# Bias and residual of a GFNet block: an fp32 home for every tile, filled by ScalarE and one accumulating DMA, and more idle matmuls before the first dense one

## The chip, the cores and the metric

The kernel runs on one core of a Trainium2 chip. A core has five engines with a queue each: TensorE (PE, with its weight loads as PEld), VectorE (DVE), ScalarE (ACT), GpSimd (POOL) and SyncE (SP), besides 16 DMA engines. Each engine works through its own queue in order and waits there on semaphores. The metric is the device time of one execution in microseconds, measured by timing whole executions. The profile comes from one further execution, which the hardware profiler recorded.

## The reference

With `x` of shape 1 x 2048 x 640 in bf16, the block is

```python
xn  = _layernorm(x)                                   # over the 640 columns
X   = rfft2(xn) * (w_r + 1j * w_i)                    # 2048 x 321 filter
y   = irfft2(X, s=(2048, 640)).astype(bfloat16)
h   = gelu(xn @ w1 + b1)                              # 640 -> 1536, tanh form
out = x + y + (h @ w2 + b2)                           # 1536 -> 640
```

## The kernel before

The 2048 rows are cut into 16 tiles of 128 rows (tile c holds the rows 16p + c, one on each partition p). The kernel has five stages, and they overlap.

1. **Norm.** DVE takes the statistics of a tile (L559, L561), POOL forms the reciprocal root (`rstd`, L564), DVE forms `nmr` (L566) and the normalised tile (`T<-X,rstd,nmr`, L587). TensorE transposes it (L599, `ps<-ident,T`), and ACT or DVE copies the result into `xnT`.
2. **First dense layer.** `ps<-xnT,W` multiplies `xnT` by `w1`; ACT applies the gelu with its bias (L645) and writes `gT`. The first two tiles go alone (128 columns), then pairs (256 columns), then two groups of four tiles (512 columns).
3. **Spectrum.** The discrete transform is written as matmuls: along the rows inside a tile (`ps<-gtab,T`, into `XV`), along the columns (`ps<-etab,XV`, into `Xb`), the remaining radix (`ps<-Xb,mtab`, into `Y`), the filter on DVE (L704, L708), and back (`ps<-Z,ntab`, into `gtab` and `T`, then a transposing DMA of SP into `XV`, L732). The stage `ps<-etab,XV` needs all 16 tiles.
4. **Back along the columns.** `ps<-getab,XV`, ACT and DVE into `Wf`, then sums and differences on DVE (L754, L759).
5. **Final sums.** For each tile the second dense layer (`ps<-W,gT`, 24 matmuls) and the last part of the inverse transform (`ps<-Wf,htab`, 2 matmuls) add up in two banks of PSUM. DVE (L819) adds an fp32 tile that holds bias plus residual, b2 + x, writes bf16 into a staging tile in `W`, and SP sends it out (L822).

Four tiles (`KEEP`) have their second dense layer done early, in the gaps of the spectrum stage. DVE then adds the bias and parks the sum in fp32 in the storage of `xnT` (L808), and an accumulating DMA on POOL adds x there (L810). For the twelve others two DMAs on POOL build b2 + x: the first writes the bias, read 128 times from HBM, into one of **three** fp32 slots in the storage of `w1` (L784), the second accumulates x on top (L785, which waits for the first to land). A slot is free for the next tile only after the DVE addition (L819) that reads it. Both DMAs wait for the end of the first dense layer, because the slots lie where `w1` was.

The order on each engine is not written by hand. A planner simulates the whole program with rough durations, picks the next operation of each engine by start time and priority, and writes the resulting order into the queues. Its priorities, `AHEAD` and `LAG` set how far the stages run ahead of one another. The order is thus fixed at build time; on the chip an engine never takes a later operation first.

At the beginning 30 matmuls on a zeroed tile (`ps<-warm`) run before any input has landed. All loads are issued by SP one after another from 0.74 us on; the bias row `b2bc` (b2, broadcast to 128 partitions) is the last of them.

Of the kernel before, what the change touches and what calls it, by code (L numbers as in the profile page):

```python
# [8 lines left out]
F32 = dt.float32  # L9
ACT = mybir.ActivationFunctionType  # L10
ALU = mybir.AluOpType

S = 2048
D = 640
# [76 lines left out]
def mm_us(n):  # L91
    return max(n / 2400.0 + 0.0027, 0.0265)
# [6 lines left out]
def act_us(n, ptr=0):  # L99
    return 0.055 + n / 1200.0 + 0.09 * ptr  # L100
# [57 lines left out]
class Sched:  # L158
# [36 lines left out]
    def schedule(self):  # L195
        free = {e: 0.75 for e in self.engines}
        dma_free = 0.0
# [22 lines left out]
        while left:  # L220
            best = None
            for e in self.engines:
                cands = []
                for o in pend[e]:
# [17 lines left out]
                    t = max(r, free[e])  # L242
# [7 lines left out]
                if e == "sp":  # L250
                    t, o = min(cands, key=lambda c: c[1].seq)
                    if o is not min((p for p in pend[e] if not p.done), key=lambda p: p.seq):
                        continue
                else:
# [4 lines left out]
                    t, o = min(near, key=lambda c: (-c[1].prio, c[1].seq))  # L259
# [4 lines left out]
            t, e, o = best  # L264
# [8 lines left out]
            if o.nbytes:  # L273
                s = max(t + 0.9, dma_free)
                dma_free = s + o.nbytes / o.rate
                o.end = dma_free + 0.9
            else:
                o.end = t + dur + LAT[e]
# [104 lines left out]
LAG = 2  # L383
KEEP = (0, 1, 4, 6)


def bass_parallel_sum__spectral_gfnet__dense_activation_gelu__prompt_kernel(
# [13 lines left out]
    xv = A_x[0].rearrange("(p c) d -> p c d", c=16)  # L401
# [4 lines left out]
    b2v = B_b2.rearrange("(o e) -> o e", o=1)  # L406

    K = Sched(nc, ["sp", "pe", "act", "dve", "pool"])
    with ExitStack() as es:
# [51 lines left out]
        p_yo, p_y2, p_yf, p_xo, p_os = Pool(2), Pool(1), Pool(2), Pool(3), Pool(4)  # L461

# [109 lines left out]
        for pair in range(8):  # L572
# [10 lines left out]
            for n in range(2):  # L583
# [13 lines left out]
                def xt(e, _, n=n, xnv=xnv, tps=tps):  # L597
                    for j in range(5):
                        ins = e.transpose(psb(tps.slot, [[1, 512]]).bitcast(BF)[:, 128 * j:128 * j + 128], xnv(n, 128 * j, [[1, 128]]), ident[:])  # L599
                    return ins  # L600
                K.op([("pe", 5 * mm_us(128))], pr, xt, reads=[B_xn, xn, B_id], writes=[tps], alts=[[("128", 5 * mm_us(128))]])
                K.op([("dve", 0.41), ("act", act_us(640))], pr,
# [139 lines left out]
        for gi, (c0, n) in enumerate(GROUPS):  # L742
# [20 lines left out]
            for i in range(n):  # L763
                c = c0 + i
                kept = c in KEEP
                xo, os_ = Buf(f"xo{c}", None if kept else p_xo), Buf(f"os{c}", p_os)
# [12 lines left out]
                def shaped(ap, kept=kept):  # L779
                    return ap.rearrange("p (j t) -> p j t", j=5) if kept else ap  # L780
                b2d = bass.AP(tensor=b2v.tensor, offset=b2v.offset, ap=[[0, 128], [1, D]])
                if not kept:
                    xb2 = Buf(f"xz{c}")
                    K.op([("pool", 1.0)], 50, lambda e, _, xov=xov: e.dma_start(xov(0, D), b2d), writes=[xo, xb2], after=free, nbytes=327680, rate=330e3)  # L784
                    K.op([("pool", 1.0)], 51, lambda e, _, c=c, xov=xov: e.dma_start(xov(0, D), xv[:, c, :], accum_op=ALU.add),  # L785
                         reads=[xb2], writes=[xo], nbytes=327680, rate=250e3)

# [16 lines left out]
                if kept:  # L804
                    kps = Buf(f"kps{c}", psum, 2, ZONE["fps"])
                    second(c, kps, 0, D, pr, [kept_ops[-2]] if len(kept_ops) > 1 else [pb_ops[-2]])
                    kx = Buf(f"kx{c}")
                    kept_ops.append(K.op([("dve", dve_us(D))], 30, lambda e, _, kps=kps, xov=xov, shaped=shaped: e.tensor_tensor(  # L808
                        out=xov(0, D), in0=shaped(psb(kps.slot, [[1, D]])), in1=shaped(b2bc[:]), op=ALU.add), reads=[kps, B_b2b], writes=[kx], after=free))
                    K.op([("pool", 1.0)], 51, lambda e, _, c=c, xov=xov, shaped=shaped: e.dma_start(xov(0, D), shaped(xv[:, c, :]), accum_op=ALU.add),  # L810
                         reads=[kx], writes=[xo], nbytes=327680, rate=250e3)
                for o0, w in [(0, D)] if c < 15 else [(0, H2), (H2, Q4), (H2 + Q4, Q4)]:
# [43 lines left out]
```

## Time and profile before

| | us |
|---|---|
| median of 3 runs | 167.04 |
| lowest and highest run | 166.98 and 167.77 |
| the profiled execution, timed | 167.08 |
| its span, first to last instruction | 165.3 |
| the time around the span | 1.8 |
| mean granted TensorE clock | 0.994 |

| engine | busy us | share of the span |
|---|---|---|
| TensorE matmul | 151.5 | 92% |
| VectorE | 112.3 | 68% |
| ScalarE | 79.9 | 48% |
| GpSimd | 30.2 | 18% |

In the timelines a row gives the start, the time to the end of the last instruction, the engine, the line, the operation with its tiles and how many were merged; the bracket is the idle time before it and what ended it. Since matmuls are pipelined, the time from one group's start to the next group's start tells their pace better than the busy time does.

### The profile page before, as it was taken

How to read it: one execution, taken by the hardware profiler on the slowest of the kernel's cores; microseconds unless marked ns; L12 is line 12 of the kernel's file. 1: busy time of each engine (PE TensorE's matmuls, PEld its weight loads, DVE VectorE, ACT ScalarE, POOL GpSimd, SP SyncE). 2: the span in 40 equal slices, each digit the busy share in tenths (PEclk: the TensorE clock that was granted, in tenths of full speed). 3: DMA queues.
4: the chain of work that ended last, by engine and by line, in shares of the span. 5: the costliest groups of instructions: out<-in, count | busy, mean ns of one | idle time of the engine just before them, and what ended most of it. 6: DMA issues, size and time to landing. Idle time of an engine off the chain costs nothing.

```text
span 165.3 us, 3751 instructions
## 1 busy us (share of the span) xinstructions
PE 151.5 (92%) x1552; PEld 100.0 (60%) x1552; DVE 112.3 (68%) x254; ACT 79.9 (48%) x146; POOL 30.2 (18%) x45
## 2 busy tenths in 40 slices
PE   7399999999999999999999999999999999998422
PEld 7199999999764545455455454756655565444312
DVE  1694999999997499898899941799964151510302
ACT  3279999899877776966483514445030010000000
POOL 1202101110020000000040333433222405125020
PEclk9999999999999999999999999999999999999997
DMA  5999999999400001822837589679897485685941
GB/s 147 356 384 396 202 160 164 159 204 367 161 0 0 0 4 40 75 48 53 111 56 107 90 154 163 124 200 269 228 204 193 102 247 127 181 207 146 236 122 40
DMA packets 29816, 25.73 MB, mean 156 GB/s; under 512 B 12520, under 2 KB 25576, under 8 KB 29800
## 3 DMA queue, kind: packets, MB, share of 16 engines
q1 hardware_dynamic: 23064, 15.66, 41.5%
q0 software_dynamic: 6080, 9.18, 25.6%
q10 hardware_dynamic: 656, 0.66, 1.1%
q8 instruction: 12, 0.20, 0.6%
q14 instruction: 4, 0.03, 0.1%
HBM read 15.66 MB, written 2.62 MB: 111 GB/s over the span
## 4 chain that ended last, share of the span: by engine, by line
PE 60%; DMA 21%; issue 6%; DVE 6%; POOL 3%; ACT 2%; SPq 1%; DVEq 0%; POOLq 0%
PE ps L469 57%; DMA W<-in_B_b_dram 16%; PE ps L599 3%; POOL W L785 3%; DMA b1t<-in_B_b_dram 3%; DMA W<-in_A_x_dram 2%; DVE W L819 2%; DVE Wf L754 1%; DVE Wf L481 1%; ACT Wf L480 1%; SPq L464 1%; DVE T L481 1%; DVE Wf L759 0%; ACT xnT L480 0%; POOL W L784 0%
## 5 line engine op out<-in xcount | busy, mean ns | idle before, releaser
L469 PE MATMUL ps<-W,gT 128*128 128x512 bf16 (+3 forms) x396 | 56.5, 295 | 7.5 <-DVE W L819 7.5
L469 PE MATMUL ps<-xnT,W 128*128 128x256 bf16 (+2 forms) x420 | 58.8, 298 | 0.8 <-ACT xnT L480 0.8
L469 PEld LDWEIGHTS ps<-W,gT 128*128 128x128 bf16 x396 | 30.1, 98 | 31.0 <-DVE W L819 9.0
L469 PEld LDWEIGHTS ps<-xnT,W 128*128 128x128 bf16 x420 | 36.9, 103 | 16.0 <-issue 1.8
L645 ACT ACTIVATE gT<-ps,b1col 128x256 bf16<-128x256 f32 (+2 forms) x84 | 39.9, 506 | 8.6 <-PE ps L469 6.4
L819 DVE TENSOR_TENSOR W<-ps,W 128x640 bf16<-128x640 f32 (+2 forms) x14 | 10.1, 728 | 28.7 <-DMA W<-in_A_x_dram 19.0
L480 ACT ACTIVATE Wf<-ps 128x960 bf16<-128x960 f32 (+1 forms) x9 | 7.9, 910 | 22.4 <-PE ps L469 22.4
L559 DVE BATCH_NORM_STATS2 stats<-X 128x6 f32<-128x320 bf16 x32 | 14.5, 476 | 3.0 <-DMA X<-in_A_x_dram 3.0
L785 POOL DMA_DIRECT2D W<-in_A_x_dram x12 | 10.4, 871 | 31.4 <-DMA W<-in_B_b_dram 31.3
L810 POOL DMA_DIRECT2D xnT<-in_A_x_dram x4 | 6.2, 1544 | 48.7 <-DVE xnT L808 48.7
L564 POOL TENSOR_TENSOR rstd<-ve,mhalf 128x2 f32<-128x2 f32 (+1 forms) x9 | 6.4, 708 | 39.9 <-DVE ve L563 39.9
L704 DVE TENSOR_TENSOR T<-Y,Wf 128x1288 bf16<-128x1288 bf16 x16 | 12.7, 825 | 0.5 <-ACT Y L480 0.2
L480 ACT ACTIVATE Xb<-ps 128x960 bf16<-128x960 f32 (+1 forms) x6 | 6.8, 1138 | 6.5 <-PE ps L469 6.5
L784 POOL DMA_DIRECT2D W<-in_B_b_dram x12 | 8.3, 751 | 7.4 <-DVE W L819 4.5
L612 DVE TENSOR_TENSOR T<-T 128x512 bf16<-128x512 bf16 (+1 forms) x32 | 8.6, 320 | 0.0
L480 ACT ACTIVATE Y<-ps 128x644 bf16<-128x644 f32 x11 | 7.4, 715 | 1.9 <-PE ps L469 1.9
L480 ACT ACTIVATE xnT<-ps 128x640 bf16<-128x640 bf16 x8 | 5.4, 704 | 5.3 <-PE ps L599 5.3
L754 DVE TENSOR_TENSOR Wf<-Wf 128x960 bf16<-128x960 bf16 (+1 forms) x12 | 6.8, 599 | 1.6 <-ACT Wf L480 1.3
L469 PE MATMUL ps<-getab,XV 32*128 32x160 bf16 (+1 forms) x128 | 7.5, 241 | 0.0
L481 DVE CAST Xb<-ps 128x960 bf16<-128x960 f32 (+1 forms) x6 | 6.7, 1123 | 1.1 <-PE ps L469 1.1
L608 DVE TENSOR_TENSOR T<-T 128x640 bf16<-128x640 bf16 x16 | 7.3, 463 | 0.0
L469 PEld LDWEIGHTS ps<-getab,XV 32*128 32x128 bf16 (+1 forms) x128 | 6.5, 146 | 1.3
(45 smaller groups left out, 144.4 us busy)
## 6 DMA issues: line engine op xcount, KB each, us to landing
W<-in_B_b_dram POOLq DMA_DIRECT2D x12, 320.0 KB, 5.4
W<-in_A_x_dram POOLq DMA_DIRECT2D x12, 320.0 KB, 4.4
out_dram<-W SPq DMA_DIRECT2D x15, 160.0 KB, 2.8
X<-in_A_x_dram SPq DMA_DIRECT2D x7, 320.0 KB, 9.5
W<-in_B_w_dram SPq DMA_DIRECT2D x1, 1920.0 KB, 15.4
W<-in_B_w_dram SPq DMA_DIRECT2D x2, 640.0 KB, 7.1
xnT<-in_A_x_dram POOLq DMA_DIRECT2D x4, 320.0 KB, 5.0
Wf<-in_A_w_r_dram SPq DMA_DIRECT2D x7, 160.5 KB, 10.9
```

Source lines behind the costliest of these rows:

```text
L469: ins = e.matmul(o_, lhsT=lw, rhs=rh, start=st, stop=sp_, skip_group_check=True)
L480: return e.activation(dst(), src(), ACT.Copy, scale=scale)
L481: return e.tensor_copy(dst(), src())
L559: K.op([("dve", 0.393)], pr, lambda e, _, c=c, h=h: e.bn_stats(stats[:, c, 6 * h:6 * h + 6], view(X, c * D + H2 * h, [[1, H2]])), reads=[B ...
L608: K.op([("dve", dve_us(640, 2))], pr, lambda e, _, k=k, op=op, xnv=xnv, x1v=x1v: e.tensor_tensor(out=x1v(H2 * k, [[D, 2], [1, H2]]), in0=x ...
L612: ring_ops.append(K.op([("dve", dve_us(4 * w, 2))], pr, lambda e, _, op=op, x1v=x1v, xfv=xfv, o_=o_, o0=o0, o1=o1, w=w: e.tensor_tensor(ou ...
L645: K.op([("act", act_us(128 * nt, 1))], pr + PRIO["gelu"], lambda e, _, c0=c0, nt=nt, fc=fc, hps=hps: e.activation(gT[:, fc, 128 * c0:128 * ...
L704: filt_ops.append(K.op([("dve", dve_us(4 * KP, 2))], pr, lambda e, _, k=k, Y=Y, TB=TB, pair=pair: e.tensor_tensor(out=view(TT, TB.slot * 8 ...
L754: K.op([("dve", dve_us(320 * n, 2))], pr + 2, lambda e, _, k=k, op=op, yo=yo, y2=y2, n=n: e.tensor_tensor(out=view(Wf, Y2 + y2.slot * 3 * ...
L784: K.op([("pool", 1.0)], 50, lambda e, _, xov=xov: e.dma_start(xov(0, D), b2d), writes=[xo, xb2], after=free, nbytes=327680, rate=330e3)
L785: K.op([("pool", 1.0)], 51, lambda e, _, c=c, xov=xov: e.dma_start(xov(0, D), xv[:, c, :], accum_op=ALU.add), reads=[xb2], writes=[xo], nb ...
L819: K.op([("dve", dve_us(w))], 95, lambda e, _, os_=os_, fps=fps, o0=o0, w=w, xov=xov, shaped=shaped, base=base: e.tensor_tensor(out=shaped( ...
```

## The change

Four things are changed together.

- The fp32 slots in the storage of `w1` are gone. Each of the 16 tiles has an fp32 home of its own, eight in the storage of `xnT` (`HOME`) and eight in that of `X`, whose bf16 input is no longer needed once both tiles there are normalised. The output staging moves to the start of `w1`'s storage.
- The bias of a tile that isn't kept is written by an ACT copy from `b2bc` (priority 5, the lowest), no longer by a DMA. One accumulating DMA on POOL then adds x. The DMA needs only the home to be free, so the planner puts most of them far ahead of the finals.
- The kept tiles are 1, 3, 5 and 7 instead of 0, 1, 4 and 6, and the planner's model of a DMA on POOL is 5 us from its issue, apart from the other queue.
- The idle matmuls at the beginning are 55 instead of 30, and 12 more stand between the first tile's transposes and the first dense matmul (`WARM`).

```diff
-KEEP = (0, 1, 4, 6)
+KEEP = (1, 3, 5, 7)
+HOME = KEEP + tuple(range(15 - (8 - len(KEEP)), 15))
+WARM = (55, 12)
...
-        xot = W1[:].bitcast(F32)
-        OST = 3 * 2 * D
+        OST = 0
...
-        B_wps = Buf("warmps", psum)
-        pe([("128", 30 * 0.108)], 300, lambda: [(psb(B_wps.slot, [[1, 128]]), warm[:], warm[:], True, True) for _ in range(30)],
-           reads=[B_warm], writes=[B_wps])
+        def idle(n, us, **kw):
+
+            b = Buf("warmps", psum)
+            pe([("128", us)], 300, lambda: [(psb(b.slot, [[1, 128]]), warm[:], warm[:], True, True) for _ in range(n)], reads=[B_warm], writes=[b], **kw)
+        idle(WARM[0], 5.25)
...
+                if not c:
+                    idle(WARM[1], WARM[1] * mm_us(128), gate=[tp])
...
-                if kept:
-                    ki = KEEP.index(c)
+                if c in HOME:
+                    ki = HOME.index(c)
                     free = [o for j, (t0, nt) in enumerate(BLOCKS) if t0 < 2 * ki + 2 for o in l1_of[j]]
...
-                    free = l1_ops
-
-                    def xov(o0, w, xo=xo):
-                        return xot[:, xo.slot * D + o0:xo.slot * D + o0 + w]
+                    ki = [b for b in range(16) if b not in HOME].index(c)
+                    free = norm_ops[:2 * ki + 2]
+
+                    def xov(o0, w, ki=ki):
+                        return X[:].bitcast(F32)[:, D * ki + o0:D * ki + o0 + w]
...
+                xb2 = Buf(f"xz{c}")
                 if not kept:
-                    xb2 = Buf(f"xz{c}")
-                    K.op([("pool", 1.0)], 50, lambda e, _, xov=xov: e.dma_start(xov(0, D), b2d), writes=[xo, xb2], after=free, nbytes=327680, rate=330e3)
-                    K.op([("pool", 1.0)], 51, lambda e, _, c=c, xov=xov: e.dma_start(xov(0, D), xv[:, c, :], accum_op=ALU.add),
-                         reads=[xb2], writes=[xo], nbytes=327680, rate=250e3)
+                    K.op([("act", act_us(D))], 5, lambda e, _, xov=xov, shaped=shaped: e.activation(xov(0, D), shaped(b2bc[:]), ACT.Copy), reads=[B_b2b], writes=[xb2], after=free)
...
+                K.op([("pool", 1.5)], 51, lambda e, _, c=c, xov=xov, shaped=shaped: e.dma_start(xov(0, D), shaped(xv[:, c, :]), accum_op=ALU.add),
+                     reads=[xb2], writes=[xo], nbytes=327680, rate=150e3)
```

What this does to the queues is seen in three places. The first is TensorE's queue at the start of the program, before the change.

```order
L469 MATMUL ps<-warm 128x128 x30
L469 MATMUL ps<-ident,b1t 128x12
L599 MATMUL ps<-ident,T 128x128 x5
L469 MATMUL ps<-xnT,W 128x128 x28
L599 MATMUL ps<-ident,T 128x128 x5
L469 MATMUL ps<-xnT,W 128x128 x57
```

And the same place after it.

```order
L473 MATMUL ps<-warm 128x128 x55
L473 MATMUL ps<-ident,b1t 128x12
L605 MATMUL ps<-ident,T 128x128 x5
L473 MATMUL ps<-warm 128x128 x12
L473 MATMUL ps<-xnT,W 128x128 x28
L605 MATMUL ps<-ident,T 128x128 x5
L473 MATMUL ps<-xnT,W 128x128 x57
```

Only idle matmuls are added here; the order of the real ones stays as it was up to the groups of 512 columns.

The second place is ACT's queue from the copy of tile 12's transpose (`xnT`), where the groups of 512 columns begin, to the first copy of the column transform (`Xb`), before the change.

```order
L480 ACTIVATE xnT<-ps 128x5x128
L645 ACTIVATE gT<-ps,b1col 128x512 x4
L480 ACTIVATE xnT<-ps 128x5x128 x2
L645 ACTIVATE gT<-ps,b1col 128x512 x2
L480 ACTIVATE XV<-ps 128x160x4
L645 ACTIVATE gT<-ps,b1col 128x512
L480 ACTIVATE Xb<-ps 128x2x2x160
```

After the change the copies of the bias (`X<-b2bc`) stand among the gelus; the piece ends with the copy of tile 15 into `XV`, which the first `ps<-etab,XV` needs.

```order
L653 ACTIVATE gT<-ps,b1col 128x512 x2
L484 ACTIVATE XV<-ps 128x160x4
L792 ACTIVATE X<-b2bc 128x640
L653 ACTIVATE gT<-ps,b1col 128x512
L792 ACTIVATE X<-b2bc 128x640
L484 ACTIVATE xnT<-ps 128x5x128
L653 ACTIVATE gT<-ps,b1col 128x512
L792 ACTIVATE X<-b2bc 128x640
L653 ACTIVATE gT<-ps,b1col 128x512
L792 ACTIVATE X<-b2bc 128x640
L484 ACTIVATE XV<-ps 128x160x4
```

Ahead of this piece stand one gelu, a bias copy, one gelu and a bias copy. So between the first gelu of 512 columns and that copy into `XV` ACT now has six bias copies, six gelus, two copies into `XV` and one into `xnT`. Six more bias copies follow later, four of them among the spectrum's copies and two after the last gelu.

The third place is POOL's queue from the first `rstd` on, before the change.

```order
L564 TENSOR_TENSOR rstd<-ve,mhalf 128x1 x2
L564 TENSOR_TENSOR rstd<-ve,mhalf 128x2 x7
L810 DMA xnT<-in_A_x_dram 128x5x128 x4
L784 DMA W<-in_B_b_dram 128x640 x3
L785 DMA W<-in_A_x_dram 128x640 x3
L784 DMA W<-in_B_b_dram 128x640 x2
L785 DMA W<-in_A_x_dram 128x640 x2
```

After the change the twelve bias DMAs are gone, and the first accumulating DMA, which waits for ACT's first bias copy, stands ahead of the last `rstd` (that of the tiles 14 and 15).

```order
L570 TENSOR_TENSOR rstd<-ve,mhalf 128x1 x2
L570 TENSOR_TENSOR rstd<-ve,mhalf 128x2 x6
L815 DMA X<-in_A_x_dram 128x640
L570 TENSOR_TENSOR rstd<-ve,mhalf 128x2
L815 DMA X<-in_A_x_dram 128x640 x7
L815 DMA xnT<-in_A_x_dram 128x5x128 x8
```

TensorE's queue has one further difference that matters below: before the first `ps<-etab,XV` it holds 45 matmuls of 512 columns instead of 38, and 75 instead of 63 before the third. So many are done earlier, and as many fewer later. In the finals the kept tiles differ, and 18 of the 24 matmuls of tile 0's second layer stand ahead of the first `ps<-getab,XV`.

More of the change, by code (lines that the diff above doesn't have):

```diff
@@ L273, in schedule @@
             if o.nbytes:
-                s = max(t + 0.9, dma_free)
-                dma_free = s + o.nbytes / o.rate
-                o.end = dma_free + 0.9
+                if e == "pool":
+                    o.end = t + 5.0
+                else:
+                    s = max(t + 0.9, dma_free)
+                    dma_free = s + o.nbytes / o.rate
+                    o.end = dma_free + 0.9
             else:
@@ L806, in bass_parallel_sum__spectral_gfnet__dense_activation_gelu__prompt_kernel @@
                     second(c, kps, 0, D, pr, [kept_ops[-2]] if len(kept_ops) > 1 else [pb_ops[-2]])
[L807 removed]
                     kept_ops.append(K.op([("dve", dve_us(D))], 30, lambda e, _, kps=kps, xov=xov, shaped=shaped: e.tensor_tensor(
[L809 to L811 removed]
+                        out=xov(0, D), in0=shaped(psb(kps.slot, [[1, D]])), in1=shaped(b2bc[:]), op=ALU.add), reads=[kps, B_b2b], writes=[xb2], after=free))
+                K.op([("pool", 1.5)], 51, lambda e, _, c=c, xov=xov, shaped=shaped: e.dma_start(xov(0, D), shaped(xv[:, c, :]), accum_op=ALU.add),
+                     reads=[xb2], writes=[xo], nbytes=327680, rate=150e3)
                 for o0, w in [(0, D)] if c < 15 else [(0, H2), (H2, Q4), (H2 + Q4, Q4)]:
```

11 lines of the change are left out of this document (5 added, 6 removed).

## The prediction

> **What bounds the kernel now.** I read the page first. It gives the span, and since TensorE is busy for 92% of it, what counts is why TensorE stands still. So the view of waits came next.
>
> ```profile
> span 165.3 us, 3751 instructions
> POOL W L785 <- DMA W<-in_B_b_dram: 31.3, 10, 4.9
> DVE W L819 <- DMA W<-in_A_x_dram: 19.0, 5, 5.5
> PE ps L469 <- DVE W L819: 7.5, 5, 3.9
> ```
>
> Read upwards, the three waits are one chain: TensorE waits for the DVE addition that frees its PSUM banks, DVE for the DMA that adds x, POOL for the bias DMA ahead of that. The chain that ended last has the same links, in order of time:
>
> ```profile
> 150.37 1.78 POOL W L785 x2
> 152.14 0.56 POOL W L784
> 152.70 4.63 issue
> ...
> 157.36 3.85 DMA W<-in_A_x_dram
> ```
>
> One tile thus costs a bias DMA (issue 0.56, 4.63 more until it is seen) and then an accumulating one (3.85), with three slots to go round. TensorE's own timeline shows where it falls behind.
>
> ```profile
> 111.56 0.99 PE L469 MATMUL ps<-W,gT 128*128 128x512 bf16 x6 [0.27 <-DVE W L819]
> 141.14 3.43 PE L469 MATMUL ps<-W,gT 128*128 128x512 bf16 x24 [0.28 <-DVE W L819]
> 148.81 3.43 PE L469 MATMUL ps<-W,gT 128*128 128x512 bf16 x24 [0.44 <-DVE W L819]
> 155.12 1.80 PE L469 MATMUL ps<-W,gT 128*128 128x320 bf16 x12 [2.60 <-DVE W L819]
> 161.84 1.00 PE L469 MATMUL ps<-W,gT 128*128 128x160 bf16 x12 [3.88 <-DVE W L819]
> ```
>
> Before 111.56 TensorE has no idle time after its first dense matmul at 8.06. So two things can move the end: the waits in the finals, and TensorE's work and waits ahead of them.
>
> **The finals.** The five waits sum to 0.27 + 0.28 + 0.44 + 2.60 + 3.88 = 7.47 us. After the change all 16 homes are separate, and 14 of the 16 accumulating DMAs can be issued before the finals begin (the last two follow the last gelu, at about 103, and their tiles 13 and 14 come 35 us later). What is late next for a bank is the DVE addition alone.
>
> ```profile
> 147.93 0.82 DVE L819 TENSOR_TENSOR W<-ps,W 128x640 bf16<-128x640 f32 x1 [4.31 <-DMA W<-in_A_x_dram]
> ```
>
> It takes 0.82, while TensorE spends about 3.5 us on a tile (24 + 2 matmuls), and two tiles' banks alternate: no wait is left in the second half. The 0.27 at 111.56 stays: there the banks wait for tile 1's addition between DVE's sums of two groups, not for a DMA, and the new order has the same wait. **Term: -7.2 us.** It could be worth less only if an addition found its home unfilled.
>
> **The start.** Here the clock matters. Rows of the timelines and of the windows:
>
> ```profile
> 0.99 3.38 PE L469 MATMUL ps<-warm 128*128 128x128 bf16 x30 [0.99 <-DVE warm L485]
> 6.43 0.19 PE L469 MATMUL ps<-ident,b1t 12*128 12x12 bf16 x1 [2.06 <-DMA b1t<-in_B_b_dram]
> 6.55 0.71 PE L599 MATMUL ps<-ident,T 128*128 128x128 bf16 x5
> 8.06 3.17 PE L469 MATMUL ps<-xnT,W 128*128 128x128 bf16 x28 [0.80 <-ACT xnT L480]
> 10.00:13.00 3.00, 3.00 (x31) 3.00 (x29) 3.00 (x12) 2.19 (x6) 0.50 (x1) 1.00 1.03 396
> 13.00:16.00 3.00, 3.00 (x55) 3.00 (x53) 1.39 (x5) 2.92 (x12) 0.44 (x1) 1.00 1.04 394
> 8.02 1.28 ACT L645 ACT_TABLE_LOAD   x1
> 11.79 0.70 ACT L480 ACTIVATE xnT<-ps 128x640 bf16<-128x640 bf16 x1 [0.48 <-PE ps L599]
> 12.40 3.67 ACT L645 ACTIVATE gT<-ps,b1col 128x128 bf16<-128x128 f32 x12
> ```
>
> The first matmuls run at half pace (28 in about 3 us), and from about 13.0 on nearly twice as many fit into three microseconds (x55 against x31): 5 us of unbroken work after 8.06, while the 3.38 us of idle matmuls with 2.06 us of nothing behind them had no effect. In the clock column of the windows (1.00 throughout) this step isn't seen; it shows in the pace alone. With 55 idle matmuls at 0.106 TensorE is busy from 0.99 to at most 6.82 and hardly stops at 6.43, so the full pace should come at about 6 to 7. The first transposes then start between 6.5 and 7.0 instead of at 6.55 and take less: within 0.3 us of before on either side, taken as 0.1 gained. ACT's table load of 1.28 follows the copy as before, and its first gelu starts at about 9.2.
>
> From there ACT is the limit, not TensorE: a narrow gelu takes 0.31 (12 in 3.67), five matmuls at full pace about 0.28. Five gelus end at 9.2 + 5 x 0.31 = 10.75, and the copy of tile 1's transpose, which before had to wait for slow matmuls until 11.79, follows at once. That is 1.0 us gained, and ACT keeps it through the rest of the narrow tiles. DVE gains more here, and from 20 on TensorE is full, so 1.0 us arrives at the groups of 512 columns: 42.8 instead of 43.80.
>
> The Trainium skill (TensorE: Matmul & The Clock Gate, section "What's actually happening") says that the full clock comes after one busy window of about 3.4 us, which runs freely against the kernel's start; the late step at 13 agrees with a window that must be busy throughout. By that figure the idle matmuls would be at full pace between 4.4 and 7.8, and the sum would change by 0.3 us at most.
>
> **The middle.** This is where the change pays. The bias copies on ACT need `b2bc`, the last load:
>
> ```profile
> 36.43 0.45 SPq L464 DMA_DIRECT2D b2bc<-in_B_b_dram  x1
> b2bc<-in_B_b_dram SPq DMA_DIRECT2D x1, 160.0 KB, 9.1
> 43.25 0.72 PE L599 MATMUL ps<-ident,T 128*128 128x128 bf16 x10
> 43.80 4.48 PE L469 MATMUL ps<-xnT,W 128*128 128x512 bf16 x20
> 48.12 0.44 PE L469 MATMUL ps<-gtab,T 128*128 128x128 bf16 x5
> 53.73 0.98 PE L469 MATMUL ps<-etab,XV 128*128 128x160 bf16 x16
> 45.08 0.69 ACT L645 ACTIVATE gT<-ps,b1col 128x512 bf16<-128x512 f32 x1 [0.53 <-PE ps L469]
> 60.07 1.25 ACT L645 ACTIVATE gT<-ps,b1col 128x512 bf16<-128x512 f32 x2
> 22.11 1.30 ACT L480 ACTIVATE XV<-ps 128x640 bf16<-128x640 f32 x2
> L480 ACT ACTIVATE Wf<-ps 128x960 bf16<-128x960 f32 x7 | 6.5, 968 | 9.2 <-PE ps L469 9.2
> ```
>
> It lands at 36.43 + 9.1 = 45.5. ACT, which is ahead of its old place, has done its first wide gelu by 44.8 and stands at the first bias copy until about 45.6. Up to the copy of tile 15 into `XV` it then has 6 bias copies, 6 wide gelus and 3 copies of 640 columns. A wide gelu costs 0.56 in a row (1.25 - 0.69), a 640-column copy 0.60 (1.30 - 0.70). The bias copy isn't in the trace; it lies between the wide gelu (0.56) and the copy of 960 columns (0.97), and I take the 640-column copy, 0.60, which has its size. So ACT ends at 45.6 + 6 x 0.60 + 6 x 0.56 + 3 x 0.60 = 54.4, and `ps<-etab,XV` starts at about 54.5. TensorE would come there at 42.8 + 45 x 0.216 + 30 x 0.055 = 54.2 (0.216 is (48.12 - 43.80)/20; 0.055 is (43.80 - 43.25)/10), so it waits 0.3.
>
> That start is later than the 53.73 of before, but 45 wide matmuls are done instead of 38: as much work as before at 54.5 - 7 x 0.216 = 53.0. **Term: -0.7 us** for start and hold together. At 0.97 a copy it would be +1.5, at 0.56 the hold would be gone and -1.0 left.
>
> Four more bias copies, 2.4 us, fall among the copies that the spectrum waits for:
>
> ```profile
> 54.00:65.00 11.00, 11.00 (x137) 5.71 (x135) 8.93 (x14) 7.27 (x11) 0.00 (x0) 1.00 0.01 2
> ```
>
> ACT is busy 7.27 of 11 us there, so its gaps could hide them, but `Y` and `T`/`gtab` copies queue behind them, and DVE (8.93) has less room. **Term: +0.3 us**, between 0 and 2.4. What hides them is the wide filler matmuls between the spectrum's stages; where it runs out, each copy's 0.6 shows in full.
>
> POOL's last `rstd` now stands behind the first accumulating DMA:
>
> ```profile
> 46.56 0.85 POOL L564 TENSOR_TENSOR rstd<-ve,mhalf 128x2 f32<-128x2 f32 x1 [4.93 <-DVE ve L563]
> 47.44 0.16 DVE L566 SCALAR_TENSOR_TENSOR nmr<-mv,rstd 128x2 f32<-128x2 f32 x1
> L785 POOL DMA_DIRECT2D W<-in_A_x_dram x12 | 10.4, 871 | 31.4 <-DMA W<-in_B_b_dram 31.3
> L810 POOL DMA_DIRECT2D xnT<-in_A_x_dram x4 | 6.2, 1544 | 48.7 <-DVE xnT L808 48.7
> 44.00:54.00 10.00, 10.00 (x72) 5.39 (x71) 8.61 (x25) 7.26 (x11) 0.85 (x1) 1.00 0.01 4
> ```
>
> The bias copy ends at 46.2; with 0.56 to 1.54 for the issue and 0.85 for `rstd`, DVE goes on at 47.6 to 48.6 and has tile 14 normalised some 0.6 later. TensorE asks for it after 28 wide matmuls, at 42.8 + 28 x 0.216 + 0.55 = 49.4. So it costs nothing, with 0.2 to 1.2 us to spare; behind `rstd` on POOL stand only DMAs that nothing wants before the finals.
>
> The Trainium skill (SBUF — State Buffer, section "SBUF: two separate sides") warns of this move: a DMA issued by GpSimd can't have its descriptors written while DVE runs an operation that takes their shared port. The DMAs leave the finals for a stretch where DVE is busy 8.61 of 10 us. The trace neither proves nor rules it out: the issues beside the busy DVE (L810) took 1.54, those in the finals 0.87, but their destinations differ in shape too. By it the issue costs the 1.54 that is in the bounds already.
>
> **The sum.** -7.2 - 0.7 + 0.3 = -7.6, and the stretch from the last matmul to the end (addition, output DMA) stays. Against the profiled execution's own 167.08 (span 165.3 and 1.8 around it; the median of the runs is 167.04, so no correction) that makes 159.4.
>
> **The rivals.**
> - *ACT becomes the bound.* The bias copies cost nearer to 0.97, or the spectrum's copies queue behind them. For: ACT's queue is full from 45.6 to 54.4. Against: a copy of 640 columns has its price in the trace. At 0.97 the middle gives +1.5 instead of -0.7, and up to 2.4 in the next stretch: 167.08 - 7.2 + 1.5 + 0.3 = 161.7, at worst 163.8.
> - *The whole slow start comes back.* TensorE ran at half pace from 8.06 to 13.0, worth 2.5 us, and 0.4 in the first transposes. If neither ACT nor the bias load holds it back: 167.08 - 7.2 - 2.9 = 157.0. Against: the gelu's 0.31 and the landing at 45.5.
> - *The waits stay in part.* The change moves the DMAs, but the last or the kept ones are still late, and one long wait (3.9) is left: 163.3. Against: 35 us between their issue and their use.
> - *Slower.* POOL holds `rstd` up: `b2bc` lands late, ACT and POOL stand at it, and tiles 14 and 15 aren't normalised when TensorE needs them. It decides once the landing is past about 46.5, and each microsecond more costs one. To undo the 7.6 gained it would have to land after 54, 168 at 55. Against: no load waits for any computation, so 45.5 should hold.
>
> **How the numbers follow.** Forecast (158.4 to 160.5, the size of the two small terms) 0.59; ACT as the bound (160.5 to 163.8) 0.18; the whole start (157.0 to 158.4) 0.16; waits left 0.04; slower 0.03. The range leaves out the outer parts of the second and third case: 157.2 to 162.2. Faster by over 0.5% (about what a measurement of this kernel can tell from no change, 0.8 us) holds in all but the last case and the worst ends: 0.94; within it 0.03; slower 0.03.
>
> **What would show it.** In the profile after: no wait of TensorE for the DVE addition above 0.4 us, and none of that addition for a DMA; the full pace of TensorE before the first dense matmul, and the copy of tile 1's transpose near 10.8; ACT's first bias copy starting at 45.6; the first `ps<-etab,XV` at 54.5 with a wait of about 0.3 for ACT. The prediction is wrong if TensorE shows waits of over 1 us in the spectrum stage, or if tile 14's transposes wait for DVE.

## The result and the profile after

The kernel after the change takes 158.05 us in the median of four runs (157.70 to 159.40), the kernel before on the same chip 167.01 (165.41 to 167.77). The ratio is 0.949, with a 95% interval of 0.940 to 0.958: faster by some 9 us. The profiled execution took 158.25 us, against 167.08. The forecast was 159.4, in a range of 157.2 to 162.2. Some executions below took over 1.5% longer than the fastest of their kernel: medians and ranges include them, ratios and their intervals do not, and the profiles of runs 7 and 10 are of such ones, so that their rows show places rather than sizes.

The page of the kernel after, and from its view of waits the rows that answer to those of before:

```profile
span 156.5 us, 3824 instructions
...
PE 152.1 (97%) x1589; PEld 100.0 (64%) x1589; DVE 113.1 (72%) x255; ACT 84.9 (54%) x157; POOL 26.0 (17%) x33
...
PE 61%; SPq 21%; ACT 6%; DMA 6%; issue 3%; DVE 2%
```

```profile
DVE W L824 <- PE ps L473: 16.4, 9, 2.7
...
ACT X L792 <- DMA b2bc<-in_B_b_dram: 0.7, 1, 0.7
```

TensorE's wait for the addition (7.5 us before) has no row any more. The addition (now L824) itself waits for TensorE, no longer for a DMA: the direction of the wait has turned round. The third row of the page is the chain that ended last. It begins with SP's issues of the loads and goes by `b2bc` and ACT's bias copies to TensorE, which is then the chain to the end.

TensorE's timeline of the kernel after, at the start and at the first matmul on `etab`:

```profile
0.99 5.58 PE L473 MATMUL ps<-warm 128*128 128x128 bf16 x55 [0.99 <-DVE warm L489]
...
7.86 1.29 PE L473 MATMUL ps<-xnT,W 128*128 128x128 bf16 x20
...
42.20 4.48 PE L473 MATMUL ps<-xnT,W 128*128 128x512 bf16 x20
...
54.01 0.98 PE L473 MATMUL ps<-etab,XV 128*128 128x160 bf16 x16 [0.25 <-ACT XV L484]
```

55 idle matmuls took 5.58 us where the half pace would take 5.8: the full pace came inside them, and the first 20 dense matmuls run at it (1.29; 28 took 3.17 before). The groups of 512 columns start at 42.20, 1.60 earlier than before. At 54.01 TensorE waits 0.25 for ACT. ACT's own rows say why:

```profile
10.62 0.70 ACT L484 ACTIVATE xnT<-ps 128x640 bf16<-128x640 bf16 x1
11.22 3.25 ACT L653 ACTIVATE gT<-ps,b1col 128x128 bf16<-128x128 f32 x12
...
43.48 0.69 ACT L653 ACTIVATE gT<-ps,b1col 128x512 bf16<-128x512 f32 x1 [0.54 <-PE ps L473]
44.85 0.74 ACT L792 ACTIVATE X<-b2bc 128x640 f32<-128x640 bf16 x1 [0.68 <-DMA b2bc<-in_B_b_dram]
45.49 0.67 ACT L653 ACTIVATE gT<-ps,b1col 128x512 bf16<-128x512 f32 x1
```

The first bias copy stands 0.68 us for its load. After it copies and gelus follow without a gap: from 44.85 to 45.49 a bias copy costs 0.64.

TensorE and DVE in the finals of the kernel after:

```profile
146.84 3.42 PE L473 MATMUL ps<-W,gT 128*128 128x512 bf16 x24
150.10 0.43 PE L473 MATMUL ps<-Wf,htab 128*128 128x512 bf16 x2
150.37 1.79 PE L473 MATMUL ps<-W,gT 128*128 128x320 bf16 x12
...
152.14 0.99 PE L473 MATMUL ps<-W,gT 128*128 128x160 bf16 x12
...
153.04 0.99 PE L473 MATMUL ps<-W,gT 128*128 128x160 bf16 x12
153.87 0.23 PE L473 MATMUL ps<-Wf,htab 128*128 128x160 bf16 x1
```

```profile
147.04 0.82 DVE L824 TENSOR_TENSOR W<-ps,xnT 128x640 bf16<-128x640 f32 x1 [2.71 <-PE ps L473]
```

No wait for the addition is left here. One remains earlier, without a bracket of its own:

```profile
112.78 2.11 PE L473 MATMUL ps<-W,gT 128*128 128x512 bf16 x12
```

Twelve such matmuls take 1.79 elsewhere (at 109.56); the 0.32 more stand where the prediction left a wait of 0.27. The last matmul starts at 153.87, before at 162.68: 8.81 us earlier.

### The profile page after: what moved, and what is told of

It reads as the page before. It is cut to its first block, busy times and chain, and to the rows that moved or that the text cites. A ratio compares the mean times of both kernels' runs of the same rounds, so it can differ in the third digit from the quotient of the medians.

```text
span 156.5 us, 3824 instructions
## 1 busy us (share of the span) xinstructions
PE 152.1 (97%) x1589; PEld 100.0 (64%) x1589; DVE 113.1 (72%) x255; ACT 84.9 (54%) x157; POOL 26.0 (17%) x33
## 4 chain that ended last, share of the span: by engine, by line
PE 61%; SPq 21%; ACT 6%; DMA 6%; issue 3%; DVE 2%
PE ps L473 61%; SPq L468 21%; DMA b2bc<-in_B_b_dram 6%; ACT X L792 2%; ACT gT L653 2%; DVE W L824 1%; DVE Wf L762 1%; ACT XV L484 1%; ACT xnT L484 0%; DVE Wf L767 0%; DVE Wf L485 0%
## 5 line engine op out<-in xcount | busy, mean ns | idle before, releaser
L473 PE MATMUL ps<-xnT,W 128*128 128x256 bf16 (+2 forms) x420 | 57.5, 288 | 0.6 <-ACT gT L653 0.4
L473 PEld LDWEIGHTS ps<-xnT,W 128*128 128x128 bf16 x420 | 34.4, 98 | 16.1 <-issue 2.9
L815 POOL DMA_DIRECT2D xnT<-in_A_x_dram x8 | 12.0, 1620 | 37.5 <-DVE xnT L813 32.5
L824 DVE TENSOR_TENSOR W<-ps,xnT 128x640 bf16<-128x640 f32 x8 | 6.5, 820 | 10.0 <-PE ps L473 10.0
L824 DVE TENSOR_TENSOR W<-ps,X 128x640 bf16<-128x640 f32 (+2 forms) x10 | 6.9, 687 | 6.5 <-PE ps L473 6.4
L484 ACT ACTIVATE Xb<-ps 128x960 bf16<-128x960 f32 (+1 forms) x7 | 8.0, 1163 | 5.5 <-PE ps L473 5.5
L815 POOL DMA_DIRECT2D X<-in_A_x_dram x8 | 7.5, 935 | 10.4 <-ACT X L792 10.4
L484 ACT ACTIVATE XV<-ps 128x640 bf16<-128x640 f32 x11 | 7.4, 705 | 0.4
L473 PE MATMUL ps<-etab,XV 32*128 32x160 bf16 (+1 forms) x128 | 7.2, 232 | 0.2 <-ACT XV L484 0.2
L473 PE MATMUL ps<-warm 128*128 128x128 bf16 x67 | 6.4, 282 | 1.0 <-DVE warm L489 1.0
```

The lines of the kernel that those rows point to most:

```text
L473: ins = e.matmul(o_, lhsT=lw, rhs=rh, start=st, stop=sp_, skip_group_check=True)
L484: return e.activation(dst(), src(), ACT.Copy, scale=scale)
L815: K.op([("pool", 1.5)], 51, lambda e, _, c=c, xov=xov, shaped=shaped: e.dma_start(xov(0, D), shaped(xv[:, c, :]), accum_op=ALU.add), reads ...
L824: K.op([("dve", dve_us(w))], 95, lambda e, _, os_=os_, fps=fps, o0=o0, w=w, xov=xov, shaped=shaped, base=base: e.tensor_tensor(out=shaped( ...
```

## The experiments

Each undoes one part of the change, does one part alone, or presses on one suspected cost. Times are medians; the ratio is to the kernel before on the same chip. On the first chip of these that kernel took 167.10, on the second 167.36, on the third 166.97.

**1. The change with 30 idle matmuls** (and one between the transposes and the first dense matmul), so without the fourth part:

```diff
-        idle(WARM[0], 5.25)
+        idle(30, 5.25)
...
-                    idle(WARM[1], WARM[1] * mm_us(128), gate=[tp])
+                    idle(1, WARM[1] * mm_us(128), gate=[tp])
```

> The changed kernel with only 30 idle matmuls at the beginning and one instead of twelve behind the first transposes; the plan, and so the order of everything else, is the same. Theory (the idle matmuls bring TensorE 1.6 us earlier to the groups of 512 columns, and the hold by the bias load and ACT's copies eats part of it): the pace of the matmuls steps up near 13 us again, the groups of 512 columns start at about 43.8 instead of 42.20, ACT's first bias copy no longer waits for its load, TensorE no longer waits for ACT at the first column transform, which starts at about 55.2 instead of 54.01. Time 1.2 us above the changed kernel, 159.3. Rival A (the whole 1.6 us were gained at the end): 159.7. Rival B (the bias load alone sets when the column transform starts, as the chain of waits says): at most 158.4.

Measured: 159.09 us (158.54 to 161.34), ratio 0.9513 (0.9465 to 0.9562). The profile's span is 157.5, against 156.5. ACT's timeline, and then TensorE's, of this run:

```profile
44.91 0.69 ACT L653 ACTIVATE gT<-ps,b1col 128x512 bf16<-128x512 f32 x1 [0.54 <-PE ps L473]
45.49 0.73 ACT L792 ACTIVATE X<-b2bc 128x640 f32<-128x640 bf16 x1
```

```profile
55.02 0.97 PE L473 MATMUL ps<-etab,XV 128*128 128x160 bf16 x16
```

The idle matmuls bring the first wide gelu forward by 1.43 us (44.91 to 43.48), and 1.01 of it reaches the first `etab` matmul (55.02 to 54.01). The other 0.42 goes to the change's wait for `b2bc`: in this run ACT comes later and does not wait. So this part is worth 1.0 us within the change, by the two profiles; the ratios (0.9513 here, 0.949 for the change) have intervals that overlap, and don't settle it.

**2. The bias load earlier in SP's queue,** ahead of `w2`:

```diff
         K.schedule()
+        sp = K.order["sp"]
+        b2 = next(o for o in sp if o.name == "b2")
+        sp.remove(b2)
+        sp.insert([o.name for o in sp].index("w2"), b2)
```

> The changed kernel with the load of the bias row moved ahead of that of the second layer's weights in SP's queue, after planning, so that every other order is the same. Theory (TensorE's own work is the bound, the hold costs only the 0.25 us that TensorE waits at the first column transform): ACT's first bias copy starts at about 44.2 instead of 44.85, the wait of TensorE for ACT there is gone, time 157.8. Rival (the chain of waits taken at its word, the bias load sets the rest): the column transform starts 0.7 us earlier and the time is 157.4. Second rival: later landing of the other loads costs something, 158.1 or more.

Measured: 159.06 (157.63 to 161.50), ratio 0.9510 (0.9440 to 0.9581), too wide to tell a few tenths. In the profile the copy no longer waits: from the first wide gelu (43.90) to the first `etab` matmul (54.01) it is 10.11 us, in the change 10.53. So the hold costs 0.42. The span is 156.5 all the same, because in this execution the 55 idle matmuls took 5.99 and everything came 0.4 later. What the load holds back is shown; that moving it pays is not.

**3. Each bias copy done twice,** one of the two into a spare tile that nothing reads (the last hunk only keeps the pairs in order):

```diff
+        spare = sb("spare", [128, D])
...
-                    K.op([("act", act_us(D))], 5, lambda e, _, xov=xov, shaped=shaped: e.activation(xov(0, D), shaped(b2bc[:]), ACT.Copy), reads=[B_b2b], writes=[xb2], after=free)
+                    K.op([("act", act_us(D))], 5, lambda e, _, xov=xov, shaped=shaped: (e.activation(spare[:], b2bc[:], ACT.Copy), e.activation(xov(0, D), shaped(b2bc[:]), ACT.Copy))[1], reads=[B_b2b], writes=[xb2], after=free)
...
+        xz = [o for o in K.order["act"] if o.name.startswith("xz")]
+        for p, o in zip(xz, xz[1:]):
+            o.deps = o.deps + [p]
```

> The changed kernel with each of ACT's twelve bias copies doubled: ahead of each stands a copy of the same row into a spare tile that nothing reads. The plan is the same. Theory (ACT has no room between the first bias copy and the first column transform): six more copies of 0.63 us move the first column transform from 54.01 to about 57.8, TensorE waits some 3.9 us there, and the four more copies in the spectrum stage cost between 0 and 2.5: 162 to 164.5. Rival (the copies lie beside other work): at most 1 us more, 159.0.

Measured: 164.29 (163.54 to 164.86), ratio 0.9838 (0.9784 to 0.9891), and a span of 161.7, 5.2 more. TensorE's waits:

```profile
PE ps L474 <- ACT XV L485: 2.1, 1, 2.1
...
PE ps L474 <- ACT gT L654: 2.0, 4, 0.8
...
PE ps L474 <- ACT gtab L485: 0.8, 1, 0.8
```

Twelve copies of 0.65 are 7.8 us of ACT work, and 5.2 of it shows. So one set of copies just fits beside TensorE's work, and a second doesn't. An ACT bound is one set of copies away.

**4. The change with the old kept tiles** (the planner orders anew, and the homes follow the list):

```diff
-KEEP = (1, 3, 5, 7)
+KEEP = (0, 1, 4, 6)
```

> The changed kernel with the kept tiles 0, 1, 4 and 6 of before; the planner orders the rest anew. Theory (which tiles are kept costs nothing, the gain is from the homes and the start): 157.7 to 158.5. Rival (the other kept tiles keep TensorE busy in the finals' first groups): a wait of TensorE for the DVE addition appears there, 159 or more.

The rival of the expectation came true: 161.13 (160.50 to 161.33), ratio 0.9645 (0.9595 to 0.9694), and a span of 158.7, 2.2 more. TensorE's timeline of this run where the finals begin, and then DVE's:

```profile
114.61 1.42 PE L473 MATMUL ps<-getab,XV 128*128 128x160 bf16 x24 [0.30 <-ACT Wf L484]
115.97 0.72 PE L473 MATMUL ps<-Wf,htab 128*128 128x512 bf16 x4
...
117.56 0.45 PE L473 MATMUL ps<-Wf,htab 128*128 128x512 bf16 x2 [0.87 <-DVE W L824]
...
118.29 2.62 PE L473 MATMUL ps<-W,gT 128*128 128x512 bf16 x17 [0.29 <-DVE W L824]
```

```profile
115.55 1.22 DVE L762 TENSOR_TENSOR Wf<-Wf 128x960 bf16<-128x960 bf16 x2
116.68 2.28 DVE L824 TENSOR_TENSOR W<-ps,xnT 128x640 bf16<-128x640 f32 x3
```

A kept tile needs only its two `htab` matmuls (0.3 us) in the finals, another tile 24 + 2 (3.5 us). With kept tiles side by side TensorE runs through them (`x4`) and then waits for DVE, whose three additions stand in a bunch behind the sums of L762. With every second tile kept, dense matmuls lie between most of the additions, and no such bracket is left. This is read from the rows; no run changes the neighbourhood alone. The waits are 1.46 us of the 2.2. Another 0.36 lies ahead of the first `etab` matmul (54.37), because `b2bc` came later in this execution, so the list is worth some 1.9 by these profiles.

**5. Before with the idle matmuls only** (`WARM` and `idle` as in the change):

```diff
+WARM = (55, 12)
...
+        idle(WARM[0], 5.25)
...
+                if not c:
+                    idle(WARM[1], WARM[1] * mm_us(128), gate=[tp])
```

> The kernel before with the idle matmuls of the change alone (55, and 12 behind the first transposes); the order of everything else is that of before. Theory (the start's gain is carried to the end, since POOL's DMAs in the finals start from the end of the first dense layer, which moves along): the groups of 512 columns start near 42.3 instead of 43.80, the waits in the finals stay at about 7.5 us, time 1.4 us below before. Rival (the DMAs in the finals set the end): the waits grow by what the start gains, time as before.

Measured: 165.63 (164.97 to 167.78), ratio 0.9922 (0.9889 to 0.9955), so 1.3 us of 167.36, with an interval of 0.8 to 1.9; the first `etab` matmul starts at 52.07 instead of 53.73. Without bias copies on ACT nothing is held back.

**6. Before with the bias written by ACT into the same three slots.** No homes, no idle matmuls, no other kept tiles, and the same order on TensorE; only the first of each pair of DMAs is replaced:

```diff
-                    K.op([("pool", 1.0)], 50, lambda e, _, xov=xov: e.dma_start(xov(0, D), b2d), writes=[xo, xb2], after=free, nbytes=327680, rate=330e3)
+                    K.op([("act", act_us(D))], 50, lambda e, _, xov=xov: e.activation(xov(0, D), b2bc[:], ACT.Copy), reads=[B_b2b], writes=[xo, xb2], after=free)
```

> The kernel before with its three slots, kept tiles and idle matmuls, but the bias written into the slot by an ACT copy instead of a DMA; TensorE's order is that of before. Theory (what made the slots too slow was the second DMA and the wait between the two on POOL; one round is then the addition 0.8, the copy 0.6, the issue 0.6 and the landing about 5, and three slots give a tile each 2.4 us, less than TensorE's 3.5): the waits of TensorE for the addition fall from 7.5 to below 1 us, time 7 us below before. Rival (three slots are too few, homes are needed): at least 3 us of the waits stay.

Measured: 158.55 (158.08 to 159.17), ratio 0.9516 (0.9457 to 0.9575). Its waits, and TensorE at the end:

```profile
DVE W L819 <- PE ps L469: 20.5, 11, 2.7
...
PE ps L469 <- DVE W L819: 0.4, 2, 0.3
```

```profile
150.56 0.43 PE L469 MATMUL ps<-Wf,htab 128*128 128x512 bf16 x2
150.83 1.79 PE L469 MATMUL ps<-W,gT 128*128 128x320 bf16 x12
...
153.43 0.23 PE L469 MATMUL ps<-Wf,htab 128*128 128x160 bf16 x1
153.50 0.99 PE L469 MATMUL ps<-W,gT 128*128 128x160 bf16 x12
```

The 7.5 us of waits are down to 0.4 with three slots as before. So the gain of the finals comes from the DMA that went, and POOL's wait between the two, not from the number of homes.

**7. The homes, with the bias by a DMA of POOL** as before, from the end of the first group of 512 columns on:

```diff
-                    K.op([("act", act_us(D))], 5, lambda e, _, xov=xov, shaped=shaped: e.activation(xov(0, D), shaped(b2bc[:]), ACT.Copy), reads=[B_b2b], writes=[xb2], after=free)
+                    b2d = bass.AP(tensor=b2v.tensor, offset=b2v.offset, ap=[[0, 128], [1, D]])
+                    K.op([("pool", 1.0)], 50, lambda e, _, xov=xov, shaped=shaped, b2d=b2d: e.dma_start(xov(0, D), shaped(b2d)), writes=[xb2], after=free + l1_of[5], nbytes=327680, rate=330e3)
```

> The changed kernel with its homes, but the bias written by a DMA on POOL from the time that the first group of 512 columns is through the first layer, in place of ACT's copies; the planner orders anew. Theory (with a home for each tile the two DMAs run far ahead of the finals, and ACT's copies cost only the hold of 0.4 us before the first column transform): no waits in the finals, the hold gone, 157.6 to 158.2. Rival (the added traffic beside SP's transposing DMAs slows the spectrum stage): waits of TensorE there, 159 or more.

Measured: 174.40 (171.83 to 179.39), ratio 1.0365 (1.0264 to 1.0465): slower than before. TensorE's timeline, then SP's queue, and a wait of DVE:

```profile
88.63 2.28 PE L473 MATMUL ps<-etab,XV 128*128 128x160 bf16 x24 [10.59 <-DVE T L485]
...
99.44 0.75 PE L473 MATMUL ps<-Xb,mtab 64*64 64x322 bf16 x8 [3.31 <-DVE gtab L485]
```

```profile
76.33 10.19 SPq L740 DMA_TRANSPOSE XV<-gtab  x2
```

```profile
DVE T L485 <- DMA XV<-T: 12.0, 2, 11.3
```

The finals have one wait of 0.8 left, though each tile has its two DMAs again: homes that are filled far ahead take these waits away too. But the DMAs of POOL now run beside the transposing DMAs of the spectrum, on which TensorE waits by way of DVE: a pair of those held SP's queue for 10.19 us, and one took 19.5 from its issue to its landing. The bias DMAs were issued from 62 us on here; whether an earlier place would cost less wasn't tried.

**8. Before with the new kept tiles:**

```diff
-KEEP = (0, 1, 4, 6)
+KEEP = (1, 3, 5, 7)
```

> The kernel before with the kept tiles 1, 3, 5 and 7 of the change; the planner orders the rest anew. In the changed kernel the old kept tiles cost about 2 us in the finals' first groups. Theory (there it counts because nothing else waits; here the DMAs' pace in the later finals absorbs it): within 0.7 us of before. Rival (the kept tiles are worth the same 2 us here): 165.

Outside both expectations: 169.26 (168.38 to 170.44), ratio 1.0139 (1.0066 to 1.0212). TensorE's waits in the finals grow to 9.3 us (8.2 for the addition, 1.1 for `Wf`), and two groups run slowly behind such waits (more on that below). So the list of kept tiles is good or bad only together with an order: worth some 1.9 us in the change, and a loss with the slots and their two DMAs.

**9. Before with ACT's copy into three slots and the idle matmuls,** that is, the edits of 5 and 6 together: the change without the homes and the new kept tiles:

```diff
+WARM = (55, 12)
...
+        idle(WARM[0], 5.25)
...
+                    idle(WARM[1], WARM[1] * mm_us(128), gate=[tp])
...
-                    K.op([("pool", 1.0)], 50, lambda e, _, xov=xov: e.dma_start(xov(0, D), b2d), writes=[xo, xb2], after=free, nbytes=327680, rate=330e3)
+                    K.op([("act", act_us(D))], 50, lambda e, _, xov=xov: e.activation(xov(0, D), b2bc[:], ACT.Copy), reads=[B_b2b], writes=[xo, xb2], after=free)
```

> The kernel before with its three slots and kept tiles, the bias written into the slot by an ACT copy, and the idle matmuls of the change; no homes. The order of all real work is that of before but for the copies. Theory (the second DMA was what the finals waited for, and the idle matmuls are worth 1.5 us where no bias copy stands ahead of the first column transform): waits in the finals below 1 us as without the idle matmuls, the first column transform near 52.1, time 1.4 us below the three slots alone and about 1 us below the changed kernel: 157.1. Rival (the homes are worth something that the three slots lack): as the changed kernel or above, 158 or more.

Measured: 157.50 (157.35 to 160.99), ratio 0.9439 (0.9393 to 0.9484), span 155.8. The first `etab` matmul starts at 52.10, and the only wait left for the addition is 0.27.

Run 4 has the same kept tiles and idle matmuls as this run, and the homes: its ratio is 0.9645 (0.9595 to 0.9694), on another chip. So with that list the homes, with the order that the planner makes for them, are slower than three slots by 2% of the time before, and the new list of kept tiles wins this back.

**10. The change with the bias copies no earlier than the end of the first group of 512 columns:**

```diff
-                    K.op([("act", act_us(D))], 5, lambda e, _, xov=xov, shaped=shaped: e.activation(xov(0, D), shaped(b2bc[:]), ACT.Copy), reads=[B_b2b], writes=[xb2], after=free)
+                    K.op([("act", act_us(D))], 5, lambda e, _, xov=xov, shaped=shaped: e.activation(xov(0, D), shaped(b2bc[:]), ACT.Copy), reads=[B_b2b], writes=[xb2], after=free + l1_of[5])
```

> The changed kernel with ACT's bias copies released only when the first group of 512 columns is through the first layer, so that none stands ahead of the first column transform; the planner orders anew, and the accumulating DMAs fall from about 60 us on, beside SP's transposing DMAs. Theory A (only the hold goes): the first column transform near 53.6, time 0.4 us below the changed kernel. Theory B (DMAs of POOL beside the transposing ones stretch these, as with the bias by DMA): SP's transposing DMAs take over 4 us a pair, TensorE waits in the spectrum stage, time 1 us or more above the changed kernel.

Measured: 160.18 (158.55 to 161.54), ratio 0.9569 (0.9510 to 0.9628). The hold ahead of `etab` is gone (52.27), and yet the span is 159.7. SP's queue in this run, then in run 9, then TensorE's waits in this run:

```profile
75.69 4.09 SPq L740 DMA_TRANSPOSE XV<-gtab  x2
79.88 4.68 SPq L740 DMA_TRANSPOSE XV<-T  x2
```

```profile
74.12 2.53 SPq L737 DMA_TRANSPOSE XV<-gtab  x2
76.75 2.92 SPq L737 DMA_TRANSPOSE XV<-T  x2
```

```profile
PE ps L473 <- DVE gtab L485: 1.6, 1, 1.6
...
PE ps L473 <- DVE W L824: 1.0, 1, 1.0
```

Of the accumulating DMAs of the twelve tiles that aren't kept, the change issues ten from 46 to 66, mostly ahead of the transposing DMAs; here they meet these in number. From issue to landing a transposing DMA took 5.1 us in the median (3.2 in run 9). The wait of 1.6 for `gtab` comes from there: DVE stood 3.64 us for a transposing DMA just before. The wait of 1.0 for the addition does not: that addition stands behind DVE's own sums in this run's new order. So the 2 us between the medians of this run and of the change are in part the place of the DMAs, in part the order. In run 9 the DMAs into the slots meet no transposing one: the first is issued at 104.96, and the last transposing DMA at 97.96.

**11. The change again,** on the chip of runs 9 and 10:

> The changed kernel once more, on the same chip as the two beside it, for the comparison: 157.7 to 159.4, with the pace step of TensorE at another time than in its first profile.

Measured: 158.04 (157.67 to 158.37), ratio 0.9467 (0.9425 to 0.9509), span 156.1. `b2bc` landed in time here (bias copy at 44.16, right behind the gelu of 43.57, no wait), and the span is 0.4 below the first profile's, which is the hold again. Run 9 is better by 0.5 us in the median, and their intervals overlap: homes and new kept tiles together add nothing that can be measured, but whether run 9 beats the change isn't settled.

## Why the prediction came out as it did

Forecast and result differ by 1.2 us of the profiled execution's time (159.44 against 158.25), in a gain of 8.8.

**The finals: the mechanism right, the size short by 0.7.** The waits that were to go went, and the addition no longer waits for a DMA. The step that was off is the sum of the brackets, "The five waits sum to ... 7.47 us", taken as the time that their removal gives. TensorE's timeline of before, ahead of the two longest waits:

```profile
152.09 0.43 PE L469 MATMUL ps<-Wf,htab 128*128 128x512 bf16 x2
...
157.72 0.23 PE L469 MATMUL ps<-Wf,htab 128*128 128x160 bf16 x1
```

From start to start the wait at 155.12 takes 3.03 us (from 152.09), and the same step in run 6, with the same order on TensorE, 0.27 (150.56 to 150.83): 2.76 saved for a bracket of 2.60. At 161.84 it is 4.12 against 0.07 (153.43 to 153.50): 4.05 for 3.88. Each wait costs 0.16 to 0.17 more than its bracket, because a bracket begins at the modelled end of the last matmul, while in an unbroken row the next one starts before that end. So the four waits that went, 7.20 us by their brackets, were worth 7.9. The fifth stayed, as predicted: 0.32 at 112.78, where the one of before cost 0.43 from start to start.

**That the homes take the waits away: true, but they aren't needed for it.** "After the change all 16 homes are separate" was given as the cause. Run 7 has the homes and two DMAs for each tile, and one wait of 0.8 in the finals. But run 6 takes the waits away with three slots: one DMA fewer in a chain of two that passes through POOL is enough. The page pointed there (31.3 us of POOL waiting for the bias DMA), and the prediction read it as a matter of slots alone.

**The start and the hold: both mechanisms right, together short by 0.5.** Predicted: groups of 512 columns at 42.8, a stop of ACT for `b2bc` until 45.6, `etab` at 54.5 with a wait of 0.3. Measured: 42.20, 44.85, 54.01 with 0.25. Two inputs were off. A narrow gelu costs ACT 0.27 (12 in 3.25), not 0.31: the 3.67 of before was itself paced by TensorE's matmuls, at first at half pace, so it was no price of ACT. And the load landed 0.7 us earlier. In the prediction's own measure, after the seven wide matmuls that moved ahead, the term is 54.01 - 1.51 - 53.73 = -1.23 instead of -0.74. The price of a bias copy, 0.60 by the copy of 640 columns, was 0.64 at most.

**The middle: right.** The last matmul starts 8.81 us earlier; 1.23 from the start and 7.9 from the finals would be 9.1. What is left over is 0.3, the price predicted for the copies among the spectrum's work. Runs 9 and 11 agree: at the first `etab` they are level (52.10 against 53.68 - 1.51 = 52.17), and the spans are 155.8 and 156.1. That it is the copies that cost these 0.3 is argued, not shown alone.

**POOL.** The first accumulating DMA took 1.05 at its issue, `rstd` followed at 46.63, and TensorE transposed tile 14 at 48.81 without a wait, as predicted.

**The kept tiles: not priced.** The prediction named the new list and gave it nothing. Run 4 puts some 1.9 us on it within the change. In the sum of before and after it doesn't appear, since it prevents waits that the new order would otherwise have. So it was luck that a choice without a price left the sum as it was: with the old list the changed kernel takes 161.13, and TensorE waits 0.87 for one addition. Why the list loses with the slots (run 8) isn't settled beyond the places of its waits.

**The rivals.** "ACT becomes the bound" did not happen, but run 3 shows how near it is. "The whole slow start comes back" would have needed an earlier `b2bc` and 2.9 us at the start; 1.6 came. "Slower", by a POOL that holds up tile 14, had the right suspect, POOL's DMAs, in the wrong place: where they did make the kernel slower (run 7), it was beside the transposing DMAs.

So the parts of the 9 us are: the bias DMA replaced by an ACT copy, nearly 8 (run 6, at the waits); the idle matmuls 1.0 (run 1), up to 1.7 where ACT is free (run 5's first `etab`); the homes with the new kept tiles nothing that can be measured (run 9).

## What to carry to other kernels

When a buffer is filled by two DMAs in a row, count the links of the chain before adding buffers: taking one link away gave here all that more buffers were meant to give. A wait read off a busy engine's timeline is best measured from start to start against the same step without a wait; and a duration taken as an engine's price must come from a place where that engine was the limit. A DMA that moves off the end must be placed where it meets no other DMA that something waits for.

## What the runs showed of the hardware

- **The pace of TensorE drops again after waits.** In run 5's profile the wait ahead of the last 12 matmuls was 4.08 us, and these then took 1.78; in the profile of before they took 1.00 behind a wait of 3.88. The window of run 5 has the clock at 0.54. In run 8 24 matmuls took 5.11 instead of 3.43 behind a wait of only 0.85; but this was the third wait within 3.2 us, and of the 3 us from 117 to 120 TensorE was busy for 1.30. Here the clock column shows the drop, unlike at the start. The end of TensorE's timeline in run 5, and the window there (the last three numbers are clock, DMA share and GB/s):

```profile
159.12 1.78 PE L470 MATMUL ps<-W,gT 128*128 128x160 bf16 x12 [4.08 <-DVE W L824]
```

```profile
158.00:162.00 4.00, 1.91 (x13) 1.59 (x13) 1.05 (x3) 0.00 (x0) 0.00 (x0) 0.54 0.12 31
```

  And in run 8, the timeline and then the window:

```profile
117.56 0.45 PE L469 MATMUL ps<-Wf,htab 128*128 128x512 bf16 x2 [1.12 <-DVE Wf L481]
118.29 0.45 PE L469 MATMUL ps<-Wf,htab 128*128 128x512 bf16 x2 [0.29 <-DVE W L819]
119.59 5.11 PE L469 MATMUL ps<-W,gT 128*128 128x512 bf16 x24 [0.85 <-DVE W L819]
```

```profile
118.00:126.00 8.00, 6.86 (x38) 3.47 (x38) 4.55 (x8) 0.00 (x0) 2.17 (x3) 0.79 0.57 164
```

  So such waits cost 0.8 us more behind them in run 5 and 1.7 in run 8. The kernel before ran at a mean clock of 0.968 to 0.993 in its 11 timed runs on the third chip, the change at 1.000 in all six. The Trainium skill (TensorE: Matmul & The Clock Gate, section "What's actually happening") has the half pace after an idle window of about 3.4 us, which runs freely. Run 5 and the row of before agree with that; in run 8 no wait is that long, and several short ones close together were enough.
- **When the full pace comes varies from run to run.** The same 55 idle matmuls took between 4.79 (run 4) and 6.03 us (run 7). With that the first dense matmul started between 7.63 (run 3) and 8.31 (run 7), and in run 2 it hid the gain.
- **Transposing DMAs of SP land later beside DMAs of POOL.** From issue to landing one took 2.6 us at the least in run 9, in the change and in run 10. The median was 3.2 in run 9, 3.8 in the change, 5.1 in run 10 beside many accumulating DMAs, and 6.1 in run 7, where bias DMAs ran too and the longest took 19.5, each in the one execution that was profiled. The time of a pair on SP's queue, as in the rows above, is the weaker sign: in the change a pair took 4.01 at 77.58, though POOL issued no DMA between 66 and 86. In the change TensorE waited for none of them. What they contend for wasn't tried.
- **The issue time of a POOL DMA followed its destination.** In the change six of the eight issues into `X` took 0.86 us each (the first two 1.05 and 1.26), while those into `xnT`, in pieces of 128 columns, took 1.5, at 63 beside a busy DVE as at 103 (three in 4.58), where DVE has little to do.
